# A fused attention and two-expert-layer kernel: gate-weight splits around the first step in another order, and two small reorderings later

## The chip, the cores and the metric

The kernel runs on one core of a Trainium2 chip. The time is the device time of one execution in microseconds (us); the number that counts is the median of the runs. A core has four compute engines that run side by side, each through its own list of instructions in order: TensorE (PE, matrix products into PSUM), VectorE (DVE), ScalarE (ACT) and GpSimd (POOL). A fifth queue, SyncE (SP), issues most of the transfers between memory and the on-chip SBUF. An instruction waits until the semaphores it names have been raised by instructions of other engines or by transfers; what is queued behind it on its engine waits with it.

## The reference

```python
attn_out = _attn_ref(x, state)                       # 4 batches, 8 heads, 512 rows + 32 states, width 64
x = attn_out.transpose(0, 2, 1, 3).reshape(B * S, H * D)   # 2176 rows of 512
x = _moe_ref(x, w_gate, w1, w2)                      # 8 experts, all of them for every row
x = _moe2_ref(x, w_gate, w_output_gate, w1, w2)      # 8 experts, the best one for each row

def _moe_ref(x, w_gate, w1, w2):
    P = np.exp(x @ w_gate - max)
    for _ in range(8):                               # rows, then columns, are normalised
        P /= P.sum(1, keepdims=True) + 1e-09
        P /= P.sum(0, keepdims=True) + 1e-09
        P *= N / E
    for e in range(E):
        out += P[:, e:e + 1] * (np.maximum(x @ w1[e], 0) @ w2[e])

def _moe2_ref(x, w_gate, w_output_gate, w1, w2):
    e_idx = np.argmax(x @ w_gate, axis=1)            # gate_w: softmax value of that expert; eom: sigmoid(x @ w_output_gate)
    for e in range(E):
        out[e_idx == e] = gate_w * eom[:, e] * (np.maximum(x[mask] @ w1[e], 0) @ w2[e])
```

All data is fp32.

## The kernel before

**Stages.** Attention comes first (blocks A0, A1 of batch 0 and C0, C1 of batch 1 ahead of everything else, the other two batches later, between matmuls). Then comes the first expert layer, which is most of the time: 17 row tiles in three passes (768, 768 and 640 rows), and in each pass 32 units (8 experts by 4 quarters of the hidden width). One unit of one pass is a step, 96 in all; `step_mm1(s)` does the first product of step s, then `step_mm2(s - 1)` the second product of the step before. The last stage (from about 1560 us) is the second expert layer: blocks of 128 rows of one expert are gathered by index, multiplied with that expert's weights (`m1`, `hT`, `m2s`) and scattered to the output.

**Precision.** A fp32 product is done as three matmuls: each operand is split into a high half (a rounded copy, on ACT) and a low half (the operand minus the high half, a subtraction on DVE or POOL). Lines 483, 484 and 485 are high x high, high x low and low x high of mm1; 565 to 567 the same of mm2.

**mm1.** A step's first product is formed from 2 x 2 quarters with seven products (Strassen's way), in the order 1, 6, 5, 7, 2, 3, 4 (in step 0 product 2 comes second). Product i takes operand `PROD[i]` of the gate weight w1 and of the rows x. The x operands x0 to x6 are made once for a pass: three quarters and four sums (`xsums`; on DVE for pass 0, L390 to L393), then split (`xsplit`: high half L405 on ACT, low half L407 on DVE or, for the numbers in `pool`, on POOL). In step 0 these operands are made just ahead of their products; the table `early` says at which gap `between(i)` (0 behind product 1, 4 behind product 2, 1, 2, 3 behind 6, 5, 7, 5 behind 3, 6 behind 4) which of them is issued. `parts[0..6]` are x0, x1, x4, x3, x5, x2, x6; product 6 uses x4, 5 uses x3, 7 uses x5, 3 uses x2, 4 uses x6. Products wait in PSUM: eight banks are used in turn, and a bank is free when the last reader (DVE's L509 to L533 or ACT's relu L492 in mm1, DVE's L583 or L574 in mm2) has read it.

**Weights.** `prep_w1(s)` gives two functions: w1a (four sums on POOL, L433 to L436, and copies on ACT, L437 and L438) and w1b (copy L441 on ACT, low halves on POOL, L443, L445 and L448 twice, then the load of the next step's w1 into the same buffer). `prep_w2(s)` copies the high half on ACT (L458), subtracts the low half on POOL (L461 twice) and then issues the load of the next step's w2. `idle_work(n)` is n small matmuls on constants that fill gaps on PE.

**What sets the order.** The order in the program is the order on each engine. Small work (attention of later batches, the second layer's routing) stands in a list `queue`; `pump(dt)`, called behind each product and tile, takes the next item when `pace` us of matmul time have gone by. `rest_(n)` are n empty items. `sel_a`, `sel_b`, `sel_c` choose the first expert of the second layer and its rows; `Rq[c]` are the routing functions fa, fb, fc (L697 to L708), ft of row chunk c. In the tail, functions are called by hand, some from inside the loops of `m1` and `m2s` (their `hooks`).

Of the kernel before, what the change touches and what calls it, by code (L numbers as in the profile page):

```python
# [21 lines left out]
def tile_state_attention_moe_moe2(  # L22
# [82 lines left out]
    def small(shape, dt=F32):  # L105
        sm_n[0] += 1
        return smp[0].tile(shape, dt, name=f"sm{sm_n[0]}")
# [286 lines left out]
        ], t  # L394

    def xsplit(p, t, order=(0, 4, 3, 5, 1, 2, 6)):
        pool = (3, 1, 6) if p > 0 else (3, 2)
        b11, b12, b21, b22, w = xquarters(p)
        of = [b11, b21, b22] + t

        def one(i):
            def f():
                hi = xop(i, 0, w).rearrange("p (k n) -> p k n", k=2)
                lo = xop(i, 1, w).rearrange("p (k n) -> p k n", k=2)
                nc.scalar.copy(hi, of[i])  # L405
                e = nc.gpsimd if i in pool else nc.vector
                e.tensor_tensor(out=lo, in0=of[i], in1=hi.bitcast(F32), op=ALU.subtract)  # L407
            return f
        return [one(i) for i in order]
# [304 lines left out]
    sel = {}  # L714
# [13 lines left out]
    def sel_a():  # L728
        npre, v, o1 = small([P, E]), small([P, E]), small([P, E])
        mxn, mm, tw, es = (small([P, 1]) for _ in range(4))  # L730
        nc.vector.tensor_copy(npre, tot[0])
        nc.vector.tensor_reduce(out=mxn, in_=npre, axis=AX.X, op=ALU.max)
        nc.vector.scalar_tensor_tensor(out=v, in0=npre, scalar=mxn, in1=rev8, op0=ALU.is_equal, op1=ALU.mult)
        nc.vector.tensor_reduce(out=mm, in_=v, axis=AX.X, op=ALU.max)
        nc.vector.tensor_scalar(out=o1, in0=rev8, scalar1=mm, scalar2=None, op0=ALU.is_equal)
        nc.vector.tensor_scalar(out=es, in0=mm, scalar1=-1.0, scalar2=float(E), op0=ALU.mult, op1=ALU.add)
        nc.vector.tensor_copy(esel[:, 0:1], es)
        nc.vector.tensor_scalar(out=tw, in0=mxn, scalar1=float(2 * P), scalar2=None, op0=ALU.is_ge)
        ie, ie2, tm = small([P, NP]), small([P, NP]), small([P, NP, E])
        nc.vector.tensor_tensor(out=tm, in0=RT["oh"][:, 0:NP, :], in1=o1.unsqueeze(1).to_broadcast([P, NP, E]), op=ALU.mult)  # L740
        nc.vector.tensor_reduce(out=ie, in_=tm, axis=AX.X, op=ALU.add)
        nc.vector.tensor_scalar(out=ie2, in0=ie, scalar1=tw, scalar2=None, op0=ALU.mult)
        bk = RT["bk"][:, 0:NP]
        os0 = small([P, NP, 2])
        osr = rtp[0].tile([P, NP, 4], FR, name="osr0")
        osg = rtp[0].tile([P, NP, 2, 2], FR, name="osg0")
        nc.vector.scalar_tensor_tensor(out=os0[:, :, 0], in0=bk, scalar=0.0, in1=ie, op0=ALU.is_equal, op1=ALU.mult)
        nc.vector.scalar_tensor_tensor(out=os0[:, :, 1], in0=bk, scalar=1.0, in1=ie2, op0=ALU.is_equal, op1=ALU.mult)
        for i, ids in enumerate((rowid, place)):
            nc.vector.tensor_tensor(out=osr[:, :, 2 * i : 2 * i + 2], in0=os0,  # L750
                                    in1=ids[:, 0:NP].unsqueeze(2).to_broadcast([P, NP, 2]), op=ALU.mult)
        sel.update(o1=o1, tw=tw, es=es, os0=os0, osr=osr, osg=osg)


    R2 = [rawb.rearrange("p a c -> p (a c)"), None, None, None]
# [156 lines left out]
    with tc.manual_schedule():  # L912
# [28 lines left out]
        w1a, w1b = prep_w1(0)  # L941
        w1a()
        A0[2]()
        A1[2]()
        C0[1]()
        idle_work(4)
        A0[3]()
        idle_work(6)
        A1[3]()
        w1b()  # L950
        C1[1]()
        C0[2]()
        A0[4]()
# [12 lines left out]
        C1[4]()  # L966
        sums[1]()

        early = {0: [parts[2], parts[3]], 4: [sums[2]], 1: [parts[4], sums[3]], 2: [parts[5], parts[6]]}

        queue = []
        credit, pace = [0.0], [1.3]
# [17 lines left out]
        def rest_(n):  # L990

            return [lambda: None] * n
# [50 lines left out]

        def step_mm1(s):
            h = PASSES[s // NU][1]
            ahead = s > 0 and s % NU == 0
            nxt = prep_w1(s + 1) if s < LAST and not ahead else [lambda: None] * 2

            def between(i):
                if s == 0:  # L1050
                    for f in early.get(i, ()):
                        f()
                    idle_work((4, 4, 4, 4, 12, 4, 0)[i])
                if i == 1 and not ahead:
                    prep_w2(s)
                if i == 3:
                    nxt[0]()
                if i == 5:
                    nxt[1]()
                pump(PITCH[h])  # L1060
            mm1(s, between)
# [37 lines left out]
        for s in range(3 * NU):  # L1099
# [8 lines left out]
                queue += [Rq[0][0]] + rest_(2) + [Rq[0][1]] + rest_(1) + [Rq[0][2]]  # L1108
                pace[0] = 3.0
            if s == 2 * NU + 1:  # L1110
                queue += [Rq[1][0]] + rest_(2) + [Rq[1][1]] + rest_(1) + [seq(Rq[1][3], sel_a)] + rest_(1) + [Rq[1][2], Rq[2][0]] + rest_(1) + [
                    sel_b] + rest_(2) + [sel_c, load_first, Rq[2][1], first_rows, Rq[2][2]]
                pace[0] = 4.0
            step_mm1(s)
# [103 lines left out]

        m1(0, (seq(A[16], Rq[3][0]), seq(Bq[15], Bq[16]), seq(Rq[4][0], Rq[3][1])))
        m1(1, (Rq[4][1], lambda: hT(0), seq(Rq[4][3], blocks, lambda: load_w(2, 0))))  # L1220
        m2s(0, (None,) * 6 + (btab, seq(lambda: gather(2), Rq[3][2], Rq[4][2], gmul)))
        hT(1)
        gather(3)
        gather(4)
        xctx.close()
# [57 lines left out]
```

## Time and profile before

| | us |
|---|---|
| median of 3 runs | 1806.25 |
| lowest and highest of them | 1804.05, 1806.64 |
| the profiled execution | 1801.52 |
| its span, first to last instruction | 1799.8 |
| PE busy | 1770.6 |
| DVE, POOL, ACT busy | 1202.5, 1126.4, 654.3 |
| mean granted clock of PE | 0.996 |

The profile is one execution of its own, a little below the runs' median. Its page has the busy time of each engine, the span in 40 slices and the groups of instructions that cost most; the trace behind it holds every instruction with its start and duration, and what ended the idle time before it, inferred from semaphores. Idle time of an engine matters only where another one waits for it. The granted clock of PE has two levels, 2.4 GHz (1.00) and 1.2 GHz (0.50); a mean between them is a share of the two.

### The profile page before, as it was taken

To read this page: it belongs to the slowest core of one execution; us is meant where nothing else is said; L and a number is where in the kernel's file an instruction comes from. 1 tells how busy PE (TensorE), PEld (TensorE's weight loads), DVE (VectorE), ACT (ScalarE), POOL (GpSimd) and SP (SyncE) were. 2 spreads that over 40 slices of the span, in tenths; PEclk is the share of its full clock that TensorE was granted. 3 is DMA by queue.
4 is the path that set the end of the run, shared out by engine and by line. 5 is a ranking of instruction groups with operands and counts; after the bars stand their busy time and mean duration, and the time that the engine had idled before them with its cause. 6 is when DMAs were issued, how large, how long until landed. Compare 5 with 4: busy or idle time off the path is not lost.

```text
span 1799.8 us, 25885 instructions
## 1 busy us (share of the span) xinstructions
PE 1770.6 (98%) x9415; PEld 1579.6 (88%) x9415; DVE 1202.5 (67%) x2054; ACT 654.3 (36%) x1114; POOL 1126.4 (63%) x1045
## 2 busy tenths in 40 slices
PE   8999999999999999999999999999999999999998
PEld 6888999999999889999999999889999998778886
DVE  6667589976666786666666666896666666635232
ACT  4433333333333433333333334333333334336333
POOL 2643566876866766666668776787878887311212
PEclk9999999999999999999999999999999999999999
DMA  5342222222222322222232223242222222434122
GB/s 123 89 111 85 79 69 71 71 74 93 68 71 68 122 70 70 70 61 69 71 100 71 71 69 96 71 141 83 82 82 83 82 76 77 138 115 176 43 92 86
DMA packets 126620, 154.67 MB, mean 86 GB/s; under 512 B 41424, under 2 KB 91600, under 8 KB 123920
## 3 DMA queue, kind: packets, MB, share of 16 engines
q1 hardware_dynamic: 122560, 142.55, 25.3%
q0 software_dynamic: 3280, 10.23, 1.8%
q8 instruction: 76, 1.25, 0.3%
q14 instruction: 64, 0.52, 0.1%
q10 hardware_dynamic: 640, 0.13, 0.0%
HBM read 138.99 MB, written 14.42 MB: 85 GB/s over the span
## 4 chain that ended last, share of the span: by engine, by line
PE 77%; issue 10%; DMA 5%; DVE 4%; POOL 2%; ACT 1%; SPq 0%; POOLq 0%; DVEq 0%; ACTq 0%
PE py L565 13%; PE py L566 13%; PE py L567 13%; PE p L483 11%; PE p L485 11%; PE p L484 11%; DMA out_dram<-xst,si 2%; DMA out_dram<-y,si 2%; PE psr L288 1%; PE psg L310 1%; DVE acc L583 1%; POOL wl L461 1%; DMA xb<-in_x_dram 1%; PE pl L612 0%; DVE HB L496 0%
## 5 line engine op out<-in xcount | busy, mean ns | idle before, releaser
L461 POOL TENSOR_TENSOR wl<-rawb,wh 128x512 fp32r<-128x512 f32 x192 | 247.5, 1311 | 395.3 <-ACT wh L458 393.7
L483 PE MATMUL p<-XR 128*128 128x384 f32 (+1 forms) x1344 | 443.7, 330 | 2.6 <-DVE acc L583 2.3
L484 PE MATMUL p<-XR 128*128 128x384 f32 (+1 forms) x1344 | 439.6, 327 | 4.5 <-POOL XR L407 3.9
L485 PE MATMUL p<-XR 128*128 128x384 f32 (+1 forms) x1344 | 439.7, 327 | 0.8 <-POOL XR L448 0.8
L565 PE MATMUL py<-wh,HB 128*128 128x512 f32 x1088 | 428.3, 394 | 1.0 <-DVE u L515 0.8
L567 PE MATMUL py<-wh,HB 128*128 128x512 f32 x1088 | 425.0, 391 | 0.0
L566 PE MATMUL py<-wl,HB 128*128 128x512 f32 x1088 | 424.9, 391 | 0.0
L583 DVE SCALAR_TENSOR_TENSOR acc<-py,PG,acc 128x512 f32<-128x512 f32 x461 | 320.3, 739 | 53.0 <-PE py L567 52.3
L448 POOL TENSOR_TENSOR XR<-sst,XR 128x512 fp32r<-128x512 f32 x192 | 273.6, 1445 | 31.1 <-ACT XR L441 29.8
L484 PEld LDWEIGHTS p<-XR 128*128 128x128 f32 x1344 | 253.2, 188 | 8.8 <-POOL XR L407 4.3
L483 PEld LDWEIGHTS p<-XR 128*128 128x128 f32 x1344 | 253.1, 188 | 7.8 <-DVE acc L583 2.7
L485 PEld LDWEIGHTS p<-XR 128*128 128x128 f32 x1344 | 252.9, 188 | 1.4 <-POOL XR L448 1.4
L565 PEld LDWEIGHTS py<-wh,HB 128*128 128x128 f32 x1088 | 204.4, 188 | 43.2 <-DVE u L515 0.9
L567 PEld LDWEIGHTS py<-wh,HB 128*128 128x128 f32 x1088 | 204.2, 188 | 43.3
L496 DVE SCALAR_TENSOR_TENSOR HB<-u,HB 128x384 fp32r<-128x384 f32 (+1 forms) x192 | 161.8, 845 | 119.1 <-ACT HB L492 118.9
L566 PEld LDWEIGHTS py<-wl,HB 128*128 128x128 f32 x1088 | 204.4, 188 | 38.7
L501 ACT COPY u<-p 128x384 f32<-128x384 f32 (+1 forms) x96 | 44.3, 461 | 462.0 <-PE p L485 461.9
L443 POOL TENSOR_TENSOR XR<-rawb,XR 128x512 fp32r<-128x512 f32 x96 | 140.3, 1461 | 0.4 <-ACT XR L437 0.4
L441 ACT CAST XR<-sst 128x1024 fp32r<-128x1024 f32 x96 | 100.7, 1048 | 101.2 <-POOL sst L436 101.1
L492 ACT ACTIVATE HB<-u 128x384 fp32r<-128x384 f32 (+1 forms) x192 | 96.8, 504 | 77.3 <-DVE u L528 72.1
L509 DVE TENSOR_TENSOR u<-p,u 128x384 f32<-128x384 f32 (+1 forms) x96 | 51.2, 533 | 93.5 <-PE p L485 93.5
L492 ACT ACTIVATE HB<-p 128x384 fp32r<-128x384 f32 (+1 forms) x96 | 45.4, 473 | 164.5 <-PE p L485 164.5
(304 smaller groups left out, 2492.0 us busy)
## 6 DMA issues: line engine op xcount, KB each, us to landing
rawb<-in_moe_w_dram SPq DMA_DIRECT2D x192, 512.0 KB, 3.5
raw<-in_moe_w_dram SPq DMA_DIRECT2D x15, 1024.0 KB, 7.9
xb<-in_x_dram SPq DMA_DIRECT2D x60, 128.0 KB, 3.5
rawb<-in_moe_w_dram SPq DMA_DIRECT2D x5, 1024.0 KB, 5.1
x1d<-acc SPq DMA_DIRECT2D x16, 256.0 KB, 4.3
xtd<-xtm SPq DMA_DIRECT2D x4, 512.0 KB, 2.7
x1p<-acc SPq DMA_DIRECT2D x8, 256.0 KB, 4.3
xst<-xtd SPq DMA_DIRECT2D x1, 1536.0 KB, 9.4
```

What stands on the lines that cost most here:

```text
L443: nc.gpsimd.tensor_tensor(out=wop(s, 1, 0, 2).rearrange(r, k=KD), in0=raw[:, :, 0:P], in1=wop(s, 0, 0, 2).rearrange(r, k=KD).bitcast(F32), ...
L448: nc.gpsimd.tensor_tensor(out=wop(s, 1, 3 + i, 2), in0=sst[:, i : i + 2, :].rearrange("p a c -> p (a c)"), in1=wop(s, 0, 3 + i, 2).bitcast ...
L461: nc.gpsimd.tensor_tensor(out=lo[:, c], in0=raw[:, c], in1=hi[:, c].bitcast(F32), op=ALU.subtract)
L483: nc.tensor.matmul(ps, wh, xh, start=start and k == 0, stop=False, skip_group_check=True)
L484: nc.tensor.matmul(ps, wh, xl, start=False, stop=False, skip_group_check=True)
L485: nc.tensor.matmul(ps, wl, xh, start=False, stop=stop and k == 1, skip_group_check=True)
L492: nc.scalar.activation(out=hh[:, f, half * h : (half + 1) * h], in_=c, func=AF.Relu)
L496: nc.vector.scalar_tensor_tensor(out=hl[:, f, q], in0=c, scalar=0.0, in1=hh[:, f, q].bitcast(F32), op0=ALU.max, op1=ALU.subtract)
L565: nc.tensor.matmul(ps, hh[:, j, r], whi[:, j, :], start=(j == 0), stop=False)
L566: nc.tensor.matmul(ps, hh[:, j, r], wlo[:, j, :], start=False, stop=False)
L567: nc.tensor.matmul(ps, hl[:, j, r], whi[:, j, :], start=False, stop=(j == 1))
L583: nc.vector.scalar_tensor_tensor(out=a, in0=ps, scalar=PG[:, t, e : e + 1], in1=a, op0=ALU.mult, op1=ALU.add)
```

## The change

It moves work in three places and takes four filler matmuls out; what is computed stays the same.

1. Around step 0: the second half of step 0's gate split (`w1b`) is issued ahead of `A1[2]` instead of behind `A1[3]`. The gate split of step 1 (`prep_w1(1)`) has its first half ahead of step 0 and its second at gap 4, behind product 2; before they stood at gaps 3 and 5 of step 0. `prep_w2(0)` moves from behind product 6 to behind product 3. The low half of x3 goes from POOL to DVE, x2's is issued earlier in the table, and one sum of x (`sums[2]`) a gap later.
2. In pass 2, `sel_a` is cut into `sel_a` (eight operations) and `sel_a2` (seven), two items of the queue; every later item comes one slot later.
3. In the tail, `Rq[3][2]`, `Rq[4][2]` (two times L697 to L708) and `gmul` (two POOL products, L1208 before) move from the last hook of `m2s(0)` to behind `hT(1)`.

```diff
     def xsplit(p, t, order=(0, 4, 3, 5, 1, 2, 6)):
-        pool = (3, 1, 6) if p > 0 else (3, 2)
+        pool = (3, 1, 6) if p > 0 else (2,)
...
         nc.vector.tensor_scalar(out=tw, in0=mxn, scalar1=float(2 * P), scalar2=None, op0=ALU.is_ge)
+        sel.update(o1=o1, tw=tw, es=es)
+
+    def sel_a2():
+        o1, tw = sel["o1"], sel["tw"]
         ie, ie2, tm = small([P, NP]), small([P, NP]), small([P, NP, E])
...
-        sel.update(o1=o1, tw=tw, es=es, os0=os0, osr=osr, osg=osg)
+        sel.update(os0=os0, osr=osr, osg=osg)
...
         A0[2]()
+        w1b()
         A1[2]()
         C0[1]()
         idle_work(4)
         A0[3]()
         idle_work(6)
         A1[3]()
-        w1b()
         C1[1]()
...
         sums[1]()
 
-        early = {0: [parts[2], parts[3]], 4: [sums[2]], 1: [parts[4], sums[3]], 2: [parts[5], parts[6]]}
+        ahead_w1 = prep_w1(1)
+        ahead_w1[0]()
+        early = {0: [parts[2]], 4: [parts[3], ahead_w1[1], parts[5]], 1: [sums[2], parts[4], sums[3]], 2: [parts[6]]}
...
-            ahead = s > 0 and s % NU == 0
+            ahead = s % NU == 0
             nxt = prep_w1(s + 1) if s < LAST and not ahead else [lambda: None] * 2
...
-                    idle_work((4, 4, 4, 4, 12, 4, 0)[i])
-                if i == 1 and not ahead:
+                    idle_work((4, 4, 4, 4, 8, 4, 0)[i])
+                if i == (1 if s > 0 else 5) and (s == 0 or not ahead):
                     prep_w2(s)
...
-                queue += [Rq[1][0]] + rest_(2) + [Rq[1][1]] + rest_(1) + [seq(Rq[1][3], sel_a)] + rest_(1) + [Rq[1][2], Rq[2][0]] + rest_(1) + [
+                queue += [Rq[1][0]] + rest_(2) + [Rq[1][1]] + rest_(1) + [seq(Rq[1][3], sel_a), sel_a2] + rest_(1) + [Rq[1][2], Rq[2][0]] + rest_(1) + [
...
-        m2s(0, (None,) * 6 + (btab, seq(lambda: gather(2), Rq[3][2], Rq[4][2], gmul)))
+        m2s(0, (None,) * 6 + (btab, lambda: gather(2)))
         hT(1)
+        Rq[3][2]()
+        Rq[4][2]()
+        gmul()
         gather(3)
```

Lines of the changed kernel behind the new function have higher numbers (L583 stays, L740 becomes L744, L878 L882, L891 L895, L1208 L1214).

The first place is POOL's list from the end of step 0's gate split (the first two lines) to the low half of step 1's w2 (`wl_615` before, `wl_611` after). Before:

```order
L445 TENSOR_TENSOR XR<-rawb,XR 128x256
L448 TENSOR_TENSOR XR<-sst,XR 128x512 x2
L407 TENSOR_TENSOR XR<-acc,XR 128x768
L461 TENSOR_TENSOR wl_522<-rawb,wh_521 128x512 x2
L407 TENSOR_TENSOR XR<-xst,XR 128x768
L433 TENSOR_TENSOR sst<-rawb 128x256
L434 TENSOR_TENSOR sst<-sst,rawb 128x256
L435 TENSOR_TENSOR sst<-rawb 128x256
L436 TENSOR_TENSOR sst<-rawb,sst 128x256
L443 TENSOR_TENSOR XR<-rawb,XR 128x512
L445 TENSOR_TENSOR XR<-rawb,XR 128x256
L448 TENSOR_TENSOR XR<-sst,XR 128x512 x2
L461 TENSOR_TENSOR wl_615<-rawb,wh_614 128x512 x2
```

With the change:

```order
L445 TENSOR_TENSOR XR<-rawb,XR 128x256
L448 TENSOR_TENSOR XR<-sst,XR 128x512 x2
L433 TENSOR_TENSOR sst<-rawb 128x256
L434 TENSOR_TENSOR sst<-sst,rawb 128x256
L435 TENSOR_TENSOR sst<-rawb 128x256
L436 TENSOR_TENSOR sst<-rawb,sst 128x256
L443 TENSOR_TENSOR XR<-rawb,XR 128x512
L445 TENSOR_TENSOR XR<-rawb,XR 128x256
L448 TENSOR_TENSOR XR<-sst,XR 128x512 x2
L407 TENSOR_TENSOR XR<-xst,XR 128x768
L461 TENSOR_TENSOR wl_577<-rawb,wh_576 128x512 x2
L461 TENSOR_TENSOR wl_611<-rawb,wh_610 128x512 x2
```

Step 1's gate split (L433 to L448) now stands ahead of x2's low half (L407 of `xst`) and of step 0's w2 split (the first pair of L461); x3's low half (L407 of `acc`) is gone from POOL.

The second place is DVE's list in pass 2, from the end of the first half of `sel_a` (L738) to the first operation of step 67's mm1 (L509); the L583 add the last three tiles of an mm2. Before:

```order
L738 TENSOR_SCALAR sm_10120<-sm_10118 128x1
L740 TENSOR_TENSOR sm_10132<-oh,sm_10117 128x64
L741 TENSOR_REDUCE sm_10130<-sm_10132 128x8
L742 TENSOR_SCALAR sm_10131<-sm_10130,sm_10120 128x8
L747 SCALAR_TENSOR_TENSOR sm_10136<-bk,sm_10130 128x8
L748 SCALAR_TENSOR_TENSOR sm_10136<-bk,sm_10131 128x8
L750 TENSOR_TENSOR osr_10137<-sm_10136,rowid 128x8x2
L750 TENSOR_TENSOR osr_10137<-sm_10136,place 128x8x2
L583 SCALAR_TENSOR_TENSOR acc<-py_14_10143,PG,acc 128x512
L583 SCALAR_TENSOR_TENSOR acc<-py_15_10151,PG,acc 128x512
L583 SCALAR_TENSOR_TENSOR acc<-py_16_10159,PG,acc 128x512
L509 TENSOR_TENSOR u_103<-p_67_10175,u_103 128x320
```

With the change:

```order
L738 TENSOR_SCALAR sm_10116<-sm_10114 128x1
L583 SCALAR_TENSOR_TENSOR acc<-py_14_10126,PG,acc 128x512
L583 SCALAR_TENSOR_TENSOR acc<-py_15_10134,PG,acc 128x512
L583 SCALAR_TENSOR_TENSOR acc<-py_16_10142,PG,acc 128x512
L744 TENSOR_TENSOR sm_10152<-oh,sm_10113 128x64
L745 TENSOR_REDUCE sm_10150<-sm_10152 128x8
L746 TENSOR_SCALAR sm_10151<-sm_10150,sm_10116 128x8
L751 SCALAR_TENSOR_TENSOR sm_10156<-bk,sm_10150 128x8
L752 SCALAR_TENSOR_TENSOR sm_10156<-bk,sm_10151 128x8
L754 TENSOR_TENSOR osr_10157<-sm_10156,rowid 128x8x2
L754 TENSOR_TENSOR osr_10157<-sm_10156,place 128x8x2
L509 TENSOR_TENSOR u_103<-p_67_10171,u_103 128x320
```

The three L583 now stand ahead of the seven operations of the second half.

The third place is DVE's list in the tail, around the scaling of block 0's result (L891, after L895) and the low halves for block 1 (L878, after L882). Before:

```order
L707 CAST gsplit<-rt_g 128x2
L708 TENSOR_TENSOR gsplit<-rt_g,gsplit 128x2
L891 TENSOR_SCALAR xst<-pY_14162,gt 128x512
L878 TENSOR_TENSOR HB<-pt_0_14242,HB 128x512
L878 TENSOR_TENSOR HB<-pt_1_14249,HB 128x512
```

With the change:

```order
L895 TENSOR_SCALAR xst<-pY_14158,gt 128x512
L882 TENSOR_TENSOR HB<-pt_0_14213,HB 128x512
L882 TENSOR_TENSOR HB<-pt_1_14220,HB 128x512
L697 TENSOR_REDUCE rt_s<-rt_d 128x3
L698 TENSOR_SCALAR rt_s<-rt_s 128x3
```

The route blocks, which ended just ahead of the scaling, now begin behind the two low halves.

## Rows read from the trace of the kernel before

**Rows 1.** The page, part 1: engine, busy us, share of the span, instructions.

```profile
PE 1770.6 (98%) x9415; PEld 1579.6 (88%) x9415; DVE 1202.5 (67%) x2054; ACT 654.3 (36%) x1114; POOL 1126.4 (63%) x1045
```

**Rows 2.** PE's waits: line, what it waited for, us in total, times, longest.

```profile
PE p L484 <- POOL XR L407: 3.9, 1, 3.9
PE pY L887 <- DVE HB L878: 3.7, 2, 3.4
PE p L483 <- DVE acc L583: 2.3, 2, 1.9
```

**Rows 3.** Windows: stretch in us, busy us of each engine, granted clock, DMA.

```profile
50.00:60.00 10.00, 9.97 (x51) 9.08 (x50) 6.80 (x10) 4.93 (x8) 10.00 (x10) 0.79 0.21 68
1150.00:1160.00 10.00, 8.10 (x44) 7.03 (x43) 9.52 (x27) 1.18 (x3) 6.84 (x8) 1.00 0.30 105
1570.00:1580.00 10.00, 9.32 (x44) 7.42 (x44) 5.99 (x6) 3.27 (x3) 4.59 (x4) 0.84 0.75 222
```

**Rows 4.** Timeline of step 0: start, us, engine, line, operation [idle before].

```profile
34.26 0.44 PE L483 MATMUL p<-XR 128*128 128x384 f32 x1
...
35.41 0.61 PE L138 MATMUL idle<-ones,onesb 128*128 128x256 bf16 x4
...
43.41 3.92 POOL L461 TENSOR_TENSOR wl<-rawb,wh 128x512 fp32r<-128x512 f32 x2 [2.75 <-ACT wh L458]
...
47.29 1.80 POOL L407 TENSOR_TENSOR XR<-xst,XR 128x768 fp32r<-128x768 f32 x1
...
49.14 0.69 PE L484 MATMUL p<-XR 128*128 128x384 f32 x1 [3.92 <-POOL XR L407]
...
53.71 0.52 PE L483 MATMUL p<-XR 128*128 128x384 f32 x1
```

**Rows 5.** POOL's timeline, then lines L448 and L407 (ns min/median/max, first and last start).

```profile
18.73 1.27 POOL L443 TENSOR_TENSOR XR<-rawb,XR 128x512 fp32r<-128x512 f32 x1 [0.45 <-ACT XR L437]
...
L448 POOL TENSOR_TENSOR XR<-sst,XR x192: 1256/1398/2011, 27.6 to 1515.2; 128x512 fp32r<-128x512 f32 x192
...
L407 DVE TENSOR_TENSOR XR<-acc,XR x3: 959/959/1059, 38.0 to 45.1; 128x768 fp32r<-128x768 f32 x3
```

**Rows 6.** Attention's second block: POOL's timeline, line L233, DVE's timeline.

```profile
27.64 2.95 POOL L448 TENSOR_TENSOR XR<-sst,XR 128x512 fp32r<-128x512 f32 x2 [6.96 <-ACT XR L441]
...
L233 DVE TENSOR_TENSOR e<-e,d x8: 691/786/1607, 20.3 to 152.7; 128x512 f32<-128x512 f32 x8
...
28.06 1.39 DVE L233 TENSOR_TENSOR e<-e,d 128x512 f32<-128x512 f32 x1
```

**Rows 7.** The page, part 6 (KB each, us to landing); PE's timeline, mm2 of step 0.

```profile
rawb<-in_moe_w_dram SPq DMA_DIRECT2D x192, 512.0 KB, 3.5
...
63.95 0.48 PE L565 MATMUL py<-wh,HB 128*128 128x512 f32 x1
```

**Rows 8.** Timelines of DVE and PE in pass 2, steps 66 to 68.

```profile
1149.77 1.13 DVE L740 TENSOR_TENSOR sm<-oh,sm 128x64 f32<-128x64 bf16 x1
...
1153.55 2.05 DVE L583 SCALAR_TENSOR_TENSOR acc<-py,PG,acc 128x512 f32<-128x512 f32 x3
...
1163.40 0.74 DVE L583 SCALAR_TENSOR_TENSOR acc<-py,PG,acc 128x512 f32<-128x512 f32 x1
...
1166.18 0.42 PE L483 MATMUL p<-XR 128*128 128x320 f32 x1 [0.45 <-DVE acc L583]
```

**Rows 9.** Timelines of DVE and POOL in the tail.

```profile
1563.49 0.17 DVE L697 TENSOR_REDUCE rt_s<-rt_d 128x3 f32<-128x24 f32 x1
...
1567.42 0.16 DVE L708 TENSOR_TENSOR gsplit<-rt_g,gsplit 128x2 fp32r<-128x2 f32 x1
...
1567.47 1.71 POOL L1208 TENSOR_TENSOR osg<-sm,gsplit 128x408 fp32r<-128x408 bf16 x2 [3.14 <-DVE gsplit L707]
...
1573.69 2.29 DVE L811 TENSOR_TENSOR setb<-raw,HB 128x2048 fp32r<-128x2048 f32 x1 [1.73 <-ACT HB L810]
...
1577.64 0.75 DVE L891 TENSOR_SCALAR y<-pY,gt 128x512 f32<-128x512 f32 x1 [1.66 <-PE pgat L719]
```

## The prediction

> **What bounds the kernel now.** I read the page's head first: TensorE (PE) is busy for 1770.6 of 1799.8 us [rows 1]. A change that leaves PE's products as they are can win only idle time of PE, 29 us in all, and what matmuls at half clock cost. So next comes the list of what PE waits for, longest first: three lines stand out, 3.9 us for a low half that GpSimd (POOL) makes (L407), 3.7 for VectorE's (DVE's) L878, 2.3 for DVE's L583 [rows 2]. Each of the three parts of the change touches one. Third, windows: the granted clock is 0.79 in 50 to 60 us and 0.84 in 1570 to 1580, right behind the first two stalls (3.92 and 3.4 us), but 1.00 in 1150 to 1160, where the stall is 1.9 [rows 2, 3]. The two long stalls so cost more than their idle time. Then the timelines of the three places.
>
> **Part 1, the start: what it takes away.** In step 0, product 3 waits from 45.2 to 49.14 for the low half of operand x2, which POOL does at 47.29 for 1.80, behind its two L461 (3.92 together) [rows 4]. From there to the first matmul of step 1 at 53.71 stand 11 matmuls and 4 fillers; at the pace of product 1 (6 matmuls in 34.26 to 35.41, 1.15) they would take about 2.5 instead of 4.57. So the stall and its half clock are worth 3.9 + 2.1 = 6.0. Now w1 of step 1 is split inside step 0 and both L461 are pushed behind x2.
>
> **What it puts in their place.** POOL and DVE cannot be counted side by side. DVE's L233, which takes 0.69 at its quickest, took 1.39 when it met POOL's L448 pair at 27.64 to 30.59 [rows 6]; operations with both operands in SBUF take turns with POOL. (The Trainium skill, SBUF, "Who interferes with whom", calls this an exclusive lock, and L233 agrees; by a plain reading without it, POOL's 6.3 us below would hide and step 1 come up to 6 us earlier.)
>
> First, L448 of step 0 moves ahead of the second block's transposes and now meets the L233 of A1, with a wait like that 0.7 there and up to 1.1 by its place in the pair; L233 of C0 and C1 run free in return. Along ACT's copies I get product 1 of step 0 at 35.0, 0.7 later than 34.26. Then the port's list up to the low half of x6, the last operand: DVE has four sums (L390 to L393) and four low halves, taken at 0.96 each, 7.7; POOL has L443 at 1.27, L445 of half that width at some 0.7, two L448 at their quickest, 1.26, and L407 at 1.8, 6.3 [rows 4, 5]. That is 14.0 of turns from 35.0, so 49.0 without a hole; I add 0.6 for moments in which DVE waits for ACT's high halves, and 0.9 for the five matmuls of product 4 behind it: step 1 begins at 50.5 instead of 53.71, a gain of 3.2. The bounds are 49.9 (no hole) and 52 (2 us of holes). Products 6, 7 and 3 each get a new wait of about one microsecond inside this time, none as long as 1.9, so I expect the clock to stay. Fillers falling from 12 to 8 cost nothing; they stood in waits.
>
> **What is late next.** prep_w2(0) moves from behind product 6 to behind product 3. Its second L461 frees the buffer for the next w2 load, so that load leaves only at 55.4 by my count and lands 3.5 later [rows 7], at 59. ScalarE (ACT) meets wh of step 1 (L458) in its list before that and waits, and queued behind it are the copies for step 2's w1, the transposed x of the third batch and the three relus of step 1. PE starts mm2 of step 0 today at 63.95 [rows 7], then at about 60.5, and around that time needs the banks that those relus and copies free. Cost: 0.3 if PE just meets them, 2 if it stands for the whole backlog; I take 0.5, because fillers of attention work lie between. Part 1: 2.7, from 1.0 to 4.5.
>
> **Part 2, the first expert's choice.** Today sel_a's 15 operations stand on DVE ahead of three L583; its second half alone lasts from 1149.77 to the L583 at 1153.55, 3.8 us, and a product waits 1.9 for the first of them [rows 2, 8]. Now the L583 stand ahead of that half, which needs nothing from them, and the 1.9 goes. All later items of the queue slide one slot. One of them is fc(1) (L697 to L708): two such blocks in the tail take from 1563.49 to 1567.6, so 2.05 each [rows 9]. It now lands between the L583 at 1163.40 and the next one. The product that today waits 0.45 at 1166.18 [rows 8] waits for that next one: it gets there some 1.9 us earlier, while the L583 ends at about 1161.5 + 0.74 + 2.05 + 0.74 = 1165.0. That wait is then 0.5 to 2.3; I take 1.35. So 1.9 + 0.45 - 1.35 = 1.0, from 0 to 1.9.
>
> **Part 3, the tail.** pY1's third matmul waits 3.4 for L878 [rows 2], which DVE holds behind the two route blocks (1563.49 to 1567.6 [rows 9]). They now come behind L878, so PE goes on at about 1565.5, and pY1, eight times three matmuls, ends near 1571. But what stands behind does not follow by as much. The gate table needs POOL's gmul (1.71 [rows 9]), which needs the route blocks, now ending at about 1570.8: it is ready at 1572 to 1574. And DVE's second L811 starts at 1573.69 when a weight load is in, which no part of the change moves, and ends at 1575.98; the scaling L891 stands behind it and starts today at 1577.64, after the table [rows 9]. So L891 can start 1.4 to 1.6 earlier and no more, and the next block's matmuls, which wait for the DVE operations behind it, with it. Part 3: 1.4. Lower bound 0.5 (gmul and L811 taking turns twice), upper 3.0 (the half clock behind the stall, 0.84 in 1570 to 1580 [rows 3], goes as well and nothing else holds it up).
>
> **Sum.** 2.7 + 1.0 + 1.4 = 5.1 of the profiled execution's 1801.52, 0.28%. The median of the runs is 1806.25, so 1806.25 x (1 - 0.0028) = 1801.2.
>
> **Rivals.**
> (a) The start gives its gain back. Either ACT's wait for the load reaches PE (2 instead of 0.5), with more holes in the port's list (2 instead of 0.6), or the clock falls in step 0 all the same. For it: four new waits lie close together where today there is one long one. Against: no stall up to 1.9 lowered the clock [rows 2, 3]. The price of the second is the 2.1 above; then the sum is 5.1 - 2.1 = 3.0 and the time 1803.2, with the first 5.1 - 2.9 = 2.2, 1804.0. (The Trainium skill, TensorE: Matmul & The Clock Gate, "What's actually happening", says that the gate follows how busy PE was lately and that its watch runs free of the kernel; by that rule neighbouring short waits can bring it down. The windows neither show nor exclude it.)
> (b) All stalls go and little comes back: 4.5 + 1.9 + 3.0 = 9.4, 1796.8. It needs every upper bound at once.
> (c) Slower: the w2 load of step 1. It sits in one queue behind loads of x and states, and the profile shows no such late one. If it lands at 66 instead of 59, PE stands for about 8 us in step 1: 8 - 3.2 = 4.8, and a stop longer than 3.9 brings the half clock, 2.1: 6.9 lost, less 2.4 of parts 2 and 3, so 4.5 slower, 1810.8. It decides from a landing at about 64 on.
> (d) The change does not do what it says: L407 of x2 is still last on POOL in step 0, behind four gate splits in place of two L461. If those run at their slow values, x2 is ready no earlier than 49; part 1 is then zero or less, and the sum 2.4 or less, 1803.8. I count it with (a).
>
> **How the numbers follow.** Forecast 50% (gain of 3.6 to 7.5), (a) with (d) 31%, (b) 9%, (c) 10%. A measurement of this kernel can tell about 0.2%, 3.6 us, from no change. Faster by more: 50 + 9 and a little of (a), 60%; within: 30%; slower: 10%. The range reaches to (b) below and over most of (a) above: 1797.0 to 1806.0.
>
> **What would show it.** Step 1's first matmul at 50 to 52 us with the clock at 1.00 throughout 40 to 60 says that the port sum was right; one behind 53 says (a) or (d). ACT's idle time before L458 of step 1, and whether PE waits for a relu's or copy's bank at 60 to 68, tells 0.5 from 2 and from (c). In pass 2, no wait at 1152, and a new one of 1 to 2 at about 1162 to 1165. In the tail, L891 right behind the second L811. The prediction fails if the three places are gained in full and some later place, which is reached with other phases of buffers and loads, gives back or adds more than 2 us.

## The result and the profile after

The changed kernel is slower: 1813.28 us median of 6 runs (1810.77 to 1817.53) against 1803.88 of 6 of the kernel before, ratio 1.0055, 95% interval 1.0040 to 1.0071. (Here and below the ratio with its interval is estimated from all runs of both kernels; it is not quite the quotient of the two medians.) Its profiled execution has a span of 1810.2 us at a mean clock of 0.991, against 1799.8 and 0.996. PE, which does 4 fillers less, is busy for longer (1778.2 us against 1770.6), because more of its matmuls ran at half clock.

PE's list of waits (line, what it waited for, us in total, times, longest):

```profile
PE p L483 <- DVE acc L583: 3.7, 2, 2.0
...
PE p L483 <- ACT u L501: 3.0, 2, 2.8
...
PE pt L878 <- issue: 2.8, 1, 2.8
...
PE pm L866 <- DVE XR L854: 2.1, 1, 2.1
```

Against [rows 2]: the wait of 3.9 us for x2's low half and the 3.4 for L878 are gone, as the change means them to be. What stands in their place is a wait of 2.8 for ACT's copy L501, 3.7 for L583 in two waits of about 2, 2.1 for the low half of a gathered block (L866), 1.3 for L574, the wait of A1 for L233 grown from 0.51 to 1.59, and 2.8 with no releaser at all ("issue") at the transposes of the last block.

Windows (stretch, busy us of PE, PEld, DVE, ACT, POOL, granted clock, DMA):

```profile
20.00:30.00 10.00, 7.50 (x37) 5.92 (x38) 6.83 (x11) 2.42 (x5) 6.14 (x7) 0.71 0.16 52
50.00:60.00 10.00, 10.00 (x62) 9.45 (x62) 8.32 (x15) 2.89 (x6) 2.86 (x2) 0.92 0.32 94
70.00:80.00 10.00, 8.52 (x44) 7.28 (x45) 8.75 (x18) 1.36 (x5) 2.54 (x2) 0.83 0.69 157
1210.00:1220.00 10.00, 6.72 (x30) 6.24 (x31) 9.62 (x20) 1.36 (x3) 6.71 (x8) 0.83 0.31 105
1570.00:1580.00 10.00, 9.00 (x47) 6.93 (x47) 7.47 (x30) 3.35 (x4) 4.34 (x5) 1.00 0.83 290
1580.00:1590.00 10.00, 7.20 (x30) 5.61 (x30) 9.07 (x8) 5.92 (x4) 7.65 (x4) 0.70 0.77 278
1790.00:1800.00 10.00, 7.16 (x29) 5.48 (x28) 2.12 (x3) 1.17 (x2) 2.05 (x2) 0.83 0.17 39
```

Against [rows 3], the clock of 50 to 60 has risen from 0.79 to 0.92 and that of 1570 to 1580 from 0.84 to 1.00. But now it is down in 20 to 30 (0.71), 70 to 80, 1210 to 1220, 1580 to 1590 and 1790 to 1800.

To see where the 10.4 us of span come from, I set the same operation of the two traces side by side, step by step (L509 of each step, then the scaling of each block, L891 before and L895 after). The lag of the changed kernel is: -1.5 us at step 1, +2.1 at step 2 and +2.2 from step 16 to step 64; +0.3 at step 67; +9.6 at step 71 and +7.8 from step 73 to the end of the passes; +4.0, +6.1 and +6.8 at the first three blocks of the tail and +6.8 up to the last but one; +10.4 at the last. So: the start loses 2.2, pass 2 loses 5.6, the tail gains 1.0, and 3.6 are lost in the last block, which the change doesn't touch.

**The start.** PE in the changed kernel: A1's transposes, the first matmul of steps 0 and 1, of mm2 of step 0, and of step 2:

```profile
23.92 0.89 PE L238 MATMUL psa<-ident,e 128*128 128x128 f32 x4 [1.59 <-DVE e L233]
...
36.26 0.44 PE L483 MATMUL p<-XR 128*128 128x384 f32 x1
...
52.43 0.33 PE L483 MATMUL p<-XR 128*128 128x384 f32 x1
...
62.13 0.48 PE L565 MATMUL py<-wh,HB 128*128 128x512 f32 x1
...
79.28 0.42 PE L483 MATMUL p<-XR 128*128 128x384 f32 x1
```

and, before, A1's transposes, step 1's copy of w2 on ACT and the first matmul of step 2:

```profile
23.10 0.66 PE L238 MATMUL psa<-ident,e 128*128 128x128 f32 x4 [0.51 <-DVE e L233]
...
55.53 1.05 ACT L458 CAST wh<-rawb 128x1024 fp32r<-128x1024 f32 x1
...
77.17 0.43 PE L483 MATMUL p<-XR 128*128 128x384 f32 x1
```

From step 0 to step 1 it now takes 16.2 us instead of 19.5 [rows 4], where the port sum put 15.5 (35.0 to 50.5). But step 0 begins 2.0 later, not 0.7: PE's wait of 1.59 in front of L238 was followed by half clock (0.71 in 20 to 30 us), which cost about 1.7, since e1 below has the same wait at full clock and begins step 0 at 34.54 instead of 36.26. And mm2 of step 0, until step 2, takes 17.2 instead of 13.2. The reason stands in the rows of DVE (x6's low half), POOL (step 0's w2), ACT (step 1's w2, then the copy L441 for step 2's w1) and PE:

```profile
50.20 0.96 DVE L407 TENSOR_TENSOR XR<-acc,XR 128x768 fp32r<-128x768 f32 x1 [0.43 <-ACT XR L405]
...
54.27 2.86 POOL L461 TENSOR_TENSOR wl<-rawb,wh 128x512 fp32r<-128x512 f32 x2 [5.78 <-ACT wh L458]
...
60.84 1.05 ACT L458 CAST wh<-rawb 128x1024 fp32r<-128x1024 f32 x1 [5.87 <-DMA rawb<-in_moe_w_dram]
...
67.97 1.05 ACT L441 CAST XR<-sst 128x1024 fp32r<-128x1024 f32 x1 [2.76 <-POOL sst L436]
...
73.61 2.07 PE L213 MATMUL pss<-sbd,xT 128*128 128x64 f32 x16 [1.32 <-DVE acc L574]
```

POOL's L461 end at 57.1; only then does the load of step 1's w2 leave, and ACT stands for 5.87 us before L458, which waited for no load before the change. The delay goes round by POOL: POOL's split of that w2 and the four sums L433 to L436 stand behind the late L458, and ACT waits for them again, 2.76, before L441. Behind L441 stands the exponential L270 of batch 2's attention, whose sum DVE awaits for 2.71 us before it gets to the L574 that frees a bank. So PE's two waits in that stretch (0.45 for L270, 1.32 for L574) are not in mm2's own matmuls but in the attention of batch 2 that runs between them; half clock follows (0.83 in 70 to 80).

**Pass 2.** DVE, ACT and PE between steps 67 and 71:

```profile
1162.41 0.17 DVE L697 TENSOR_REDUCE rt_s<-rt_d 128x4 f32<-128x32 f32 x1
...
1166.66 0.17 DVE L644 TENSOR_REDUCE rt_mx<-L 128x4 f32<-128x32 f32 x1
...
1167.87 0.23 ACT L650 ACTIVATE rt_d<-rt_d 128x32 f32<-128x32 f32 x1 [7.39 <-DVE rt_d L649]
...
1168.58 0.42 PE L483 MATMUL p<-XR 128*128 128x320 f32 x1 [2.78 <-ACT u L501]
...
1185.92 0.15 DVE L788 COPY sm<-pgat 128x4 f32<-128x4 f32 x1
...
1191.95 0.48 DVE L533 TENSOR_TENSOR u<-u,p 128x320 f32<-128x320 f32 x1
...
1196.73 0.20 DVE L667 TENSOR_REDUCE rt_ck<-oh 128x8 f32<-128x32 bf16 x1
...
1201.75 0.49 DVE L509 TENSOR_TENSOR u<-p,u 128x320 f32<-128x320 f32 x1
...
1206.27 4.60 DVE L496 SCALAR_TENSOR_TENSOR HB<-u,HB 128x320 fp32r<-128x320 f32 x2
...
1211.59 0.42 PE L483 MATMUL p<-XR 128*128 128x320 f32 x1 [2.01 <-DVE acc L583]
...
1217.73 0.41 PE L483 MATMUL p<-XR 128*128 128x320 f32 x1 [1.69 <-DVE acc L583]
```

and fb(2) before, from its first operation to the L583 behind it:

```profile
1191.20 0.19 DVE L667 TENSOR_REDUCE rt_ck<-oh 128x8 f32<-128x32 bf16 x1
...
1193.55 2.06 DVE L583 SCALAR_TENSOR_TENSOR acc<-py,PG,acc 128x512 f32<-128x512 f32 x3
```

The wait of 1.9 at 1152 is gone. The first new one is 2.78 at 1165.8 to 1168.6: fc(1) and three L583 now stand ahead of fa(2) on DVE (1162.41 to 1166.66), two small exponentials of fa(2) wait on ACT for it (L650, 7.39 idle), and L501, which frees a bank, stands behind them on ACT. Then sel_c (1185.92 to 1191.95, 6.0 us) sits between the last two products of step 69's mm1, and fb(2) (1196.73 to 1201.75, 5.0 us) ahead of the L509 of step 70; before, they took 5.3 and 2.4 in other places. DVE runs behind from there: its last two L496 of step 70 fall beside POOL's L448 and L461 and take 4.60 together (0.48 and 1.30 before). PE waits 2.01 for the L583 behind them and 1.69 for an L583 that stands behind fc(2) (1212.11 to 1216.93), and the clock goes down (0.83 in 1210 to 1220).

**The tail and the end.** DVE, then PE, around the second scaling:

```profile
1572.53 1.29 DVE L882 TENSOR_TENSOR HB<-pt,HB 128x512 fp32r<-128x512 f32 x2 [0.30 <-ACT HB L881]
...
1581.57 2.29 DVE L815 TENSOR_TENSOR setb<-raw,HB 128x2048 fp32r<-128x2048 f32 x1 [0.16 <-ACT HB L814]
...
1583.77 0.75 DVE L895 TENSOR_SCALAR y<-pY,gt 128x512 f32<-128x512 f32 x1
...
1585.51 0.80 PE L866 MATMUL pm<-HB,XR 128*128 128x512 f32 x1 [2.12 <-DVE XR L854]
```

L882 now comes ahead of the route blocks and the scaling (1583.77) starts right behind the second L815 (it ends at 1583.86), as forecast. But half clock has not left the tail: behind a new wait of 2.12 for L854 it is 0.70 in 1580 to 1590. The last block, and the page's row of the queue that loads instructions (76 packets in the kernel before):

```profile
1795.40 1.59 PE L878 MATMUL pt<-ident,xst 128*128 128x128 f32 x8 [2.84 <-issue]
...
q8 instruction: 77, 1.26, 0.3%
```

The trace shows no semaphore that PE waits for here; it stands for 2.84 us and then runs at half clock (0.83 in 1790 to 1800). These transposes belong to `finish`, which stands in both arms of a branch that is decided at run time (`with tc.If(nbv > lo)`, L1253), so PE comes to them by way of a branch. The Trainium skill, "Runtime: NRT & Kernel Launch", section "Instruction fetch mechanics", says that instructions are fetched ahead in sequence, and that a taken branch to code outside the pages at hand makes the engine wait for a fetch. The trace agrees in part: one packet of the instruction queue falls into the stop, from 1792.45 to 1793.86. But PE resumes 1.5 us after its end, and the 77th packet starts only 1.1 us behind the stop (1796.53); the kernel before goes through the same branch without a stop, with a packet from 1785.87 to 1787.39 while PE works. So a wait for code is argued, not shown.

### The profile page after: what moved, and what is told of

Its sections match the earlier page's. It is cut to its first block, busy times and chain, and to the rows that moved or that the text cites. A ratio compares the mean times of both kernels' runs of the same rounds, so it can differ in the third digit from the quotient of the medians.

```text
span 1810.2 us, 25870 instructions
## 1 busy us (share of the span) xinstructions
PE 1778.2 (98%) x9411; PEld 1584.2 (88%) x9411; DVE 1210.7 (67%) x2055; ACT 653.8 (36%) x1114; POOL 1128.5 (62%) x1044
## 4 chain that ended last, share of the span: by engine, by line
PE 77%; issue 10%; DVE 5%; DMA 5%; POOL 2%; ACT 1%; SPq 0%; POOLq 0%; DVEq 0%; ACTq 0%
PE py L565 13%; PE py L566 13%; PE py L567 13%; PE p L483 11%; PE p L485 11%; PE p L484 11%; DMA out_dram<-xst,si 2%; DMA out_dram<-y,si 2%; PE psr L288 1%; DVE HB L496 1%; PE psg L310 1%; DVE acc L583 1%; PE pss L213 1%; POOL wl L461 1%; PE pl L612 0%
## 5 line engine op out<-in xcount | busy, mean ns | idle before, releaser
L461 POOL TENSOR_TENSOR wl<-rawb,wh 128x512 fp32r<-128x512 f32 x192 | 246.5, 1306 | 408.7 <-ACT wh L458 407.2
L583 DVE SCALAR_TENSOR_TENSOR acc<-py,PG,acc 128x512 f32<-128x512 f32 x461 | 320.5, 739 | 52.5 <-PE py L567 51.9
L448 POOL TENSOR_TENSOR XR<-sst,XR 128x512 fp32r<-128x512 f32 x192 | 273.2, 1442 | 23.5 <-ACT XR L441 23.4
L496 DVE SCALAR_TENSOR_TENSOR HB<-u,HB 128x384 fp32r<-128x384 f32 (+1 forms) x192 | 163.4, 853 | 119.6 <-ACT HB L492 119.4
L501 ACT COPY u<-p 128x384 f32<-128x384 f32 (+1 forms) x96 | 44.4, 463 | 457.0 <-PE p L485 457.0
L441 ACT CAST XR<-sst 128x1024 fp32r<-128x1024 f32 x96 | 100.7, 1049 | 108.1 <-POOL sst L436 108.0
L509 DVE TENSOR_TENSOR u<-p,u 128x384 f32<-128x384 f32 (+1 forms) x96 | 51.2, 534 | 91.7 <-PE p L485 88.9
```

Of the source, the lines that this page charges most:

```text
L448: nc.gpsimd.tensor_tensor(out=wop(s, 1, 3 + i, 2), in0=sst[:, i : i + 2, :].rearrange("p a c -> p (a c)"), in1=wop(s, 0, 3 + i, 2).bitcast ...
L461: nc.gpsimd.tensor_tensor(out=lo[:, c], in0=raw[:, c], in1=hi[:, c].bitcast(F32), op=ALU.subtract)
L496: nc.vector.scalar_tensor_tensor(out=hl[:, f, q], in0=c, scalar=0.0, in1=hh[:, f, q].bitcast(F32), op0=ALU.max, op1=ALU.subtract)
L583: nc.vector.scalar_tensor_tensor(out=a, in0=ps, scalar=PG[:, t, e : e + 1], in1=a, op0=ALU.mult, op1=ALU.add)
```

## The experiments

**The three parts alone.** e1 makes only part 1, e2 only part 2, e3 only part 3 of the diff. e4 is e2 with the empty item behind `sel_a2` taken out, so that nothing behind it moves:

```diff
-[seq(Rq[1][3], sel_a), sel_a2] + rest_(1) + [Rq[1][2], Rq[2][0]]
+[seq(Rq[1][3], sel_a), sel_a2] + [Rq[1][2], Rq[2][0]]
```

e1, expected: 

> Only part 1 (the splits around step 0) is made. Theory S (read from the trace of the changed kernel): L448 ahead of the second block's transposes blocks A1's L233, PE then waits 1.6 us and runs at half clock from 24 to 31 us; the load of w2 for step 1 comes late as well; by the trace of the whole change step 2 begins 2.2 us later than before, so this kernel is 2 to 3 us slower than the one before (ratio 1.0011 to 1.0017). Rival: the start is neutral or faster alone (gain 2.7 as predicted) and what was lost there in the whole change is chance of one execution: ratio 0.9985.

Measured: 1805.40 against 1803.45, ratio 1.0018 (1.0007 to 1.0029). The number is theory S's, the reason is not. The trace lags by -3.2 at step 1, +0.3 at step 2, -1.05 from step 3 on, -1.4 in the tail, and +2.2 at the last block. The last block's transposes in e1, where the instruction queue has 77 packets as well:

```profile
1784.13 0.27 PE L874 MATMUL pt<-ident,xst 128*128 128x128 f32 x1
1786.98 0.98 PE L874 MATMUL pt<-ident,xst 128*128 128x128 f32 x7 [2.58 <-issue]
```

So the start was faster by 1 us in this execution (its clock was 1.00 in 20 to 30, although L238 waited 1.6 here too), and the loss is the stop at the end, 3.65 with the half clock behind it. The first matmuls of step 1, of mm2 of step 0 and of step 2 repeat the two halves of the start:

```profile
50.46 0.33 PE L483 MATMUL p<-XR 128*128 128x384 f32 x1
...
60.16 0.48 PE L565 MATMUL py<-wh,HB 128*128 128x512 f32 x1
...
76.04 0.42 PE L483 MATMUL p<-XR 128*128 128x384 f32 x1
```

15.9 us from step 0 (34.54) to step 1, and 15.9 from mm2 to step 2, against 19.5 and 13.2 before.

e2, expected: 

> Only part 2 (sel_a in two items of the queue, all later items one slot later). Theory M: the slot shift puts sel_c and the ranks of chunk 2 into worse places of steps 69 to 72, which costs 7.5 us, while the wait of 1.9 at 1152 goes; net 5 to 6 us slower, ratio 1.003. Rival: the loss of the whole change in these steps comes from its start, whose shift of phases reaches pass 2; then this kernel is 0 to 2 us faster than before.

Measured: 1809.74 against 1803.45, ratio 1.0036 (1.0023 to 1.0049): theory M. The three new waits stand as in the whole change, 2.77 for L501 and then 2.01 and 1.71 for L583; the first, which half clock follows here (0.83 in 1170 to 1180):

```profile
1170.55 0.41 PE L483 MATMUL p<-XR 128*128 128x320 f32 x1 [2.77 <-ACT u L501]
```

Between step 64 and the end of the passes its trace loses 7.2 us.

e3, expected: 

> Only part 3 (the route blocks and the gate product behind the next block's low halves). Theory T: 1.0 us faster, as the trace of the whole change shows between the first and the third scaling of the tail, and the stop of 2.8 us of PE ahead of the last block's transposes, which the profile puts down to no releaser, is not bound to this edit; ratio 0.9994. Rival: that stop comes with this edit; then 2.5 us slower, ratio 1.0014, and the trace shows the stop.

Measured: 1801.11 against 1803.45, ratio 0.9996 (0.9987 to 1.0004). The interval holds theory T's 0.9994 and no change, but not the rival's 1.0014; the trace has no stop at the end and is 2.2 us ahead from the third block on.

e4, expected: 

> Part 2 with the empty item behind it taken out, so that every later item of the queue keeps the slot that it has in the kernel before. Theory M: the wait of 1.9 at 1152 goes and nothing else moves, 1.5 to 1.9 us faster, ratio 0.999. Rival: the seven operations in their new place cost as much as they save (the product that waits for the next L583 loses it again): no change.

Measured: 1801.05, ratio 0.9992 (0.9982 to 1.0002). The trace gains 1.9 at step 67 and gives 1.3 back by step 68, in short waits for L448 (0.79) and L583 (0.47). So the cut of sel_a is worth about 0.6 us in the trace, and the interval holds no change; the shift of the rest by one slot is what costs: without it 1.0036 becomes 0.9992.

**The stop at the end.** e1 and the whole change have it, e2, e3 and e4 do not. Part 1 takes 4 fillers out of PE's list (`idle_work((4, 4, 4, 4, 12, 4, 0)[i])` to 8). e5 makes that one edit in the kernel before, e6 gives part 1 alone its 12 fillers back.

e5, expected: 

> The kernel before with one number changed: 8 fillers instead of 12 behind product 2 of step 0. Nothing that the multiplications wait for is touched. Theory F: the stop of 2.6 us of PE ahead of the last block's transposes, which the kernel with part 1 alone and the whole change both show and the kernels with part 2 or part 3 alone do not, hangs on the number of PE's instructions (8 fewer), that is on where its code lies when PE branches to the last block; then this kernel shows the stop and the half clock behind it and is 3 to 4 us slower, ratio 1.002. Rival: the stop comes with the data flow of part 1; then no change, ratio 1.000, and no stop.

Measured: 1801.59 against 1802.24, ratio 1.0000 (0.9991 to 1.0010), no stop in the trace, and the instruction queue has 76 packets as before. Theory F as it was put failed.

e6, expected: 

> Part 1 alone, but with the 12 fillers of the kernel before, so that PE has as many instructions as before. Theory F: no stop at the end; what is left of part 1 is what its trace showed between step 3 and the last stage, 1.0 us faster, ratio 0.9994, against 1.0018 with 8 fillers. Rival: the stop stays, ratio 1.0015 to 1.002.

Measured: 1803.89 against 1802.24, ratio 1.0008 (0.9997 to 1.0018); no stop in the trace. The time is not theory F's, whose 0.9994 lies below the interval; the rival's 1.0015 lies inside, but its cause, the stop, isn't there. What this execution has instead is half clock behind A1's wait of 1.59 (0.83 in 20 to 30): step 0 begins at 36.18 against e1's 34.54, and the trace is 0.45 behind the kernel before from step 3 on, where e1 was 1.05 ahead. The lengths of PE's instruction list in the built programs may tell why e5 has no stop: part 1 also takes a few semaphore entries from it, so that e5's is longer (10058 entries) than e1's (10054); the kernel before has 10066, e6 10063. e9 therefore takes the kernel before down to e1's length, with 6 fillers.

e9, expected: 

> The kernel before with 6 fillers instead of 12 in that one place: PE's list is then as long as that of the kernel with part 1 alone, which shows the stop ahead of the last block (10054 entries; the whole change 10055, stop; 8 fewer fillers' entries, 10058, none; part 1 with 12 fillers, 10064, none). Theory F, now with a bound between 10055 and 10058: this kernel shows the stop of 2.6 us and the half clock behind it, 3 to 4 us slower, ratio 1.002. Rival: the stop needs the data flow of part 1; no stop, ratio 1.000.

Measured: 1806.68 against 1802.25, ratio 1.0026 (1.0014 to 1.0038), and

```profile
PE pt L874 <- issue: 2.7, 1, 2.7
...
q8 instruction: 77, 1.26, 0.3%
```

Its trace is within 0.1 us of the kernel before at all steps and blocks but the last, where it is 5.0 behind. So the stop comes with the length of PE's list, not with the data flow of part 1. Its place says the same: in e1 and e9, with 10054 entries, PE stands behind the first of the eight transposes; in the whole change, with 10055, it stands ahead of the first, whose weights are already loaded. One entry more in front, and the stop falls one instruction sooner: it is bound to a place in the list.

e10, expected: 

> The whole change with 12 fillers instead of 8, nothing else. Theory F: no stop at the end, so 3 to 4 us of the whole change's 10 are gone: ratio 1.0035. Rival: the fillers have no part in it, 1.0055 as the whole change.

Measured: 1812.23 against 1802.25, ratio 1.0048 (1.0031 to 1.0065). The stop is gone from the trace, but the median is nearer to the rival's number, and the interval holds both. Its trace shows where the gain was hidden: pass 2 loses 8.6 us in this execution instead of 5.6 (7.2 in e2's), with the same waits, of which one is longer and one is followed by half clock at once (0.64 for the first matmul; 0.83 in 1160 to 1170, where the whole change had 1.00):

```profile
1166.16 0.64 PE L483 MATMUL p<-XR 128*128 128x320 f32 x1 [2.77 <-ACT u L501]
...
1216.69 0.42 PE L483 MATMUL p<-XR 128*128 128x320 f32 x1 [3.25 <-DVE acc L583]
```

**The load of w2.** e7 and e8 are e6 with prep_w2(0) at another gap:

```diff
-                if i == (1 if s > 0 else 5) and (s == 0 or not ahead):
+                if i == (1 if s > 0 else 2) and (s == 0 or not ahead):   (e7; 1 in e8)
```

e7, expected: 

> As the one before (part 1 alone, 12 fillers), with prep_w2(0) behind product 5 (gap 2) instead of behind product 3 (gap 5). Theory W: of the 3.2 us that part 1 gains up to step 1, 3.5 are lost between step 1 and step 2, since the late load of step 1's w2 holds ScalarE for 5.9 us; three us earlier, the load costs about 1 less, so 2 to 3 us faster than before, ratio 0.9985. Rival: the loss there is the second batch of attention's own chain, which does not depend on the load; then the same as e6, 0.9994.

Measured: 1800.20 against 1802.24, ratio 0.9990 (0.9981 to 0.9999).

e8, expected: 

> As e7, with prep_w2(0) behind product 6 (gap 1), where the kernel before has it; the low half of x2 still stands ahead of it on GpSimd. Theory W: ScalarE's wait for the load goes nearly whole, but GpSimd's two L461 then take turns with the sums for x6, up to 1.3 us: 2.5 to 4 us faster than before, ratio 0.998 to 0.9986. Rival: the turns cost as much as the earlier load saves, the same as e6, 0.9994.

Measured: 1800.16, ratio 0.9995 (0.9985 to 1.0005). PE's first matmuls of mm2 of step 0 and of step 2, and ACT's L458 of step 1 in e8:

```profile
61.41 0.48 PE L565 MATMUL py<-wh,HB 128*128 128x512 f32 x1
...
74.63 0.43 PE L483 MATMUL p<-XR 128*128 128x384 f32 x1
...
55.61 1.05 ACT L458 CAST wh<-rawb 128x1024 fp32r<-128x1024 f32 x1 [1.33 <-DMA rawb<-in_moe_w_dram]
```

From mm2 to step 2 it is 13.2 us again, as before the change, in e7 too (62.69 to 75.91); ACT's wait is 1.33. With the late load it is 15.5 (e6) to 17.2 (the whole change). So the loss in mm2 of step 0 is the late load, and theory W holds for it. The times alone would not decide it: e7's interval holds the theory's 0.9985 and the rival's 0.9994, e8's holds 0.9994 and only the edge of the theory's range (0.9986). They moved by less than the theory gave: in both kernels L238 still waits 1.6, and their clock is 0.68 (e7) and 0.77 (e8) in 20 to 30.

**Put together.** e11 has all three parts, with 12 fillers, prep_w2(0) behind product 6 and the queue of e4; e12 also has `w1b()` behind `A1[3]()` again.

e11, expected: 

> The three parts together, each without what made it slow: 12 fillers, prep_w2(0) behind product 6, sel_a2 without a shift of the later items, and part 3 as it is. By the sum of the single ones (0.9995, 0.9992, 0.9996): 3 to 5 us faster than before, ratio 0.998. Rival: part 3 and the rest overlap (one clock window in the tail), 2 us, 0.999.

Measured: 1798.07 against 1802.25, ratio 0.9979 (0.9967 to 0.9990).

e12, expected: 

> As e11, with the second half of step 0's gate split behind A1[3] again, where the kernel before has it. Theory C: the L448 pair beside A1's L233 lengthens PE's wait there to 1.6 us, after which the clock is often down (granted 0.68 to 0.83 in 20 to 30 us in four of five such kernels); without it the clock stays at 1.00 there and the start gains 1 to 2 us more: ratio 0.997 to 0.998. Rival: C1 pays the same on the other side, no difference to e11.

Measured: 1796.94 against 1802.25, ratio 0.9966 (0.9955 to 0.9977): 5 us faster than the kernel before, and by the two ratios some 0.9% faster than the changed one. e11 and e12 differ in the direction of theory C, but their intervals overlap, and e12's profile can't decide it: it has a clock of 0.55 in 10 to 20 us, ahead of anything that was edited:

```profile
10.00:20.00 10.00, 9.91 (x52) 9.45 (x53) 3.79 (x6) 2.05 (x4) 2.82 (x4) 0.55 0.91 204
```

## Why the prediction was wrong

I predicted 1801.2 (1797.0 to 1806.0), a gain of 5.1. It is a loss of 9.4 us between the medians and of 10.4 between the two profiled executions. The step that failed most is the term of part 2: it put the shift of the queue at one wait of 1.35 and left the items behind fc(1) at nothing, where 5.0 of the 7.5 us lost in pass 2 fall (1.9 are gained). The term of the start came out at -2.2 instead of +2.7, through a stall behind ACT's late load that was mis-sized and half clock that was not expected, and 3.6 us were lost in a place that the sum doesn't have.

- **The port sum of part 1 was nearly right.** It put step 1 15.5 us behind step 0; it is 16.2 in the whole change and 15.9 in e1, from 19.5 before. That step 1 begins at 50.46 in e1, as forecast (50.5), is partly luck, since step 0 begins 0.5 earlier than forecast there; in the whole change the late step 0 moves it to 52.43.
- **"I expect the clock to stay": failed, but at another place.** I priced the waits in step 0. The half clock came at A1's L238, whose wait I had put at 0.7 to 1.1 for L233's delay without adding the 0.5 that PE waits there anyway: 1.6. It cost about 1.7 us there in the whole change, and in e6, e7, e8 and e11 the window also shows it (0.68 to 0.83); e1 and e10 have the same wait at clock 1.00. So the same wait is followed by half clock in some executions and not in others. My rule from the rows, that no stall up to 1.9 lowers the clock, rested on one stall, and the kernel before itself speaks against it: its clock is down from about 1580 to 1583 as well, behind a wait of 0.68 (L860, 1578.87). The window is next to the one in [rows 3]:

```profile
1580.00:1590.00 10.00, 8.60 (x32) 6.64 (x31) 5.28 (x3) 5.42 (x5) 1.04 (x1) 0.84 0.36 129
```

- **"What is late next" named the right wait and mis-sized it.** I gave ACT's wait for the w2 load a cost of 0.5, at most 2. It is 2.3 (e6) to 3.9 (whole change) between mm2 of step 0 and step 2; moving the load back in front takes all of it away (e7, e8). I had priced only the banks that PE needs at once. What I left out is that POOL's split and sums and the next batch's attention, which runs inside mm2, hang on the same copy. "Fillers of attention work lie between" was my reason for the small price; it is these that PE waited in.
- **Part 2 stopped one item too early.** I followed the queue's shift to fc(1) and one product, where a wait of 0.5 to 2.3 was forecast and 2.8 measured, by way of an ACT copy behind two exponentials that I had left out. The items behind it (sel_c, fb(2), fc(2)) I did not follow at all, and there most of the loss is: in step 71, behind them, PE's lag grows by 5.0. A gain of 1.0 was forecast, and 5.6 were lost (e2 alone: ratio 1.0036; the shift taken out: 0.9992).
- **Part 3 was nearly right by the trace.** L895 starts right behind the second L815, the tail gains 1.0 of the forecast 1.4 in the whole change and 2.1 in e3's trace; e3's interval does not set it apart from no change. That the wait for L854 would come up in place of the one for L878, with half clock behind it, was not forecast.
- **The stop at the end was in none of my cases.** It costs 3.6 to 5.0 us and hangs on the length of PE's list (e9). "Fillers falling from 12 to 8 cost nothing" holds in step 0 (e5: 1.0000), but they are part of what shortened the list: with 12 of them the stop is gone (e6, e10).
- **The rivals.** The slower one, (c), has the right sign and nearly the right time, 1810.8, and the right load; but it asked for a landing at 66, and the load landed at 60.8. That its time is near is luck. A rival for part 2, "the later items fall into worse places", was missing, though the change's own text (every later item one slot later) called for it. The last sentence of the prediction, on a later place that takes back more than 2 us, names what happened in kind, but it had no price and no chance.

The sum that the runs leave: part 1 at 12 fillers 1.0008 (e6), the stop alone 1.0026 (e9), part 2 1.0036 (e2), part 3 0.9996 (e3), together 1.0066, which lies inside the interval of the whole change (1.0040 to 1.0071). Without the stop the same sum gives 1.0040, inside e10's interval (1.0031 to 1.0065). Taking the stop off the whole change's own ratio gives 1.0029, a little outside it. Pass 2 loses 5.6, 7.2 and 8.6 us in the three profiles that have the shift; in the two larger ones half clock follows the wait for L501. Why it follows in some executions and not in others stays open.

## What to carry to other kernels

When an item is put into a paced queue, follow every item behind it to the end of the queue, on each engine that it uses; what moves can cost more than the edit gives (here 1.0036 with the shift, 0.9992 without). Price a late operand by all that stands behind the waiting instruction on its engine, not only by the reader that comes first. And compare a change with one that only pads or shortens an engine's list, before a loss in an untouched place is put down to data flow.

## What the runs showed of the hardware that I had not expected

- PE stands for 2.6 to 2.8 us at the last block's first transpose (ahead of it or behind it), with no releaser in the profile, in the kernels whose PE list has 10054 or 10055 entries (whole change, e1, e9), and not in those with 10058 or more (before, e2 to e8 and e10 to e12). In the three with the stop the instruction queue moved 77 packets instead of 76, the last of them 1.1 us behind the stop. A wait for code is what this suggests; it was not shown apart from that, and why some lengths have it was not tried.
- The granted clock in 10 to 20 us, where nothing had been edited, was 0.54 and 0.55 in the profiles of e2 and e12 and 1.00 in all others; e2's execution was 4.2 us behind by step 0, though e2 edits nothing ahead of it. One profile is therefore no measure of a start.
- Short operations on DVE grew with the place that they fell into: the ten of fb(2) took 2.4 us before, next to POOL's gathers, and 5.0 after, next to its splits and sums; the ten of sel_c 5.3 and 6.0, next to splits and sums both times.
